# Output projection of a gated attention and feed-forward kernel: fp32r products with TensorE transposes, against scaled fp16 products with transposing DMAs

## The chip, the cores and the metric

The kernel runs on one core of one Trainium2 chip. The metric is device time in microseconds, the median of several runs. Besides the runs there is one profiled execution with a trace of every instruction and DMA packet; its own time is given below. TensorE multiplies matrices, VectorE, ScalarE and GpSimd work elementwise, and SyncE's queue issues nearly all DMAs. Profiles name them PE (PEld for its weight loads), DVE, ACT, POOL and SP. A matmul reads its operands from SBUF and accumulates in one of eight PSUM banks.

## The reference

With S = 2048 tokens, D = 576 channels, 32 heads of 18 channels, four segments of 512 tokens and F = 4608 hidden channels:

```python
g = sigmoid((x * gate_w).sum(-1, keepdims=True))
# attention branch: per segment, causal softmax attention inside the segment and a running
# memory (M, z) of the segments before; sb = sigmoid(beta), one per head
o = sb * (phi(q) @ M) / (phi(q) @ z + 1e-6) + (1 - sb) * softmax(q k^T * scale + mask) @ v
a = o @ wo
b = (silu(x @ w_gate) * (x @ w_up)) @ w_down      # feed-forward branch
out = g * a + (1 - g) * b
```

Everything is fp32 in the reference. The kernel keeps near that precision by splitting each operand into a high and a low part in a short format and adding three products (high x high, high x low, low x high).

## The kernel before, in words

**Stages.** First come the projections q, k, v and the memory branch, segment by segment; the memory branch's rows (already weighted by sigmoid(beta)) go to a DRAM array `med`, one row of 576 per token. Then the feed-forward branch runs for the two halves of the tokens (`half` 0 and 1), each over 36 tiles of hidden channels (`f`), so 72 *positions*; the attention of 64 units of two heads is woven into it and writes its rows to the DRAM array `atd`. Last comes the output stage: for 16 tiles of 128 tokens, in the order segments 2, 3, 0, 1, it forms o = `atd` + `med` (segment 0 has no `med`), multiplies by `wo`, and merges with the feed-forward rows.

**A position of the feed-forward loop.** Seven groups of seven matmuls (`seven`, lines 1388 and 1391) with steps of ScalarE and VectorE between them. L1471 copies the first group's PSUM bank for further accumulation, L1494 is a SiLU, L1500 and L1501 multiply gate and up parts, L1260 and L1263 split the result in `hh` and `hl` for the down projection. After each group, and one extra time, stands a `tick`, eight a position, numbered 0 to 7. A tick issues DMAs of its own (`dw`, line 1149), then one *beat*: it runs whatever was deferred to this beat, then some down-projection groups (9 matmuls each, line 1160, accumulated on VectorE at L1169), then a step of the attention. `defer(k, fn)` puts a function into the k-th beat from now. Down groups come in sixteens after every third f, so positions come in threes: one long, with the groups, and two short. The sixteen groups of the last three f are left over for the output stage. Weights for the next position (line 864, `wo__` tiles of a pool, not the matrix wo) and their remainder (line 355) are fetched through SyncE's queue one position ahead.

**Queues.** The order on every engine and queue is the program's order, written out by hand; no scheduler moves it. An instruction whose inputs are not ready holds what is behind it on its engine. This holds for SyncE's queue too: a DMA that waits for its source or for a free buffer holds the DMAs behind it. In the second half the attention turns part of its units with transposing DMAs (`turn`, line 950), of 128 x 1024 fp16, in that same queue.

**Opening the output stage.** When the attention is through, in beat 6 of the third position from the end, `c_open` closes its pools and opens the pool `cp`. It spreads six loads of parts of `wo` (line 1204, into the four staging buffers of `raw_tile`) over the next nine beats; five beats after each load ScalarE copies the high part (L1207), seven beats after, VectorE takes the low part (L1208), which frees the staging buffer. `c_load` (lines 1213, 1217) fetches `atd` and `med` rows of tile 0 in beat 2 and of tile 1 in beat 6.

**The output stage.** Seventeen rounds (line 1538). Round n loads tile n+2 and its feed-forward rows (`f_load`, for tiles 0 to 7; the others are still in SBUF), prepares tile n (`c_tr`), runs two left-over down groups (four in round 0), and multiplies tile n-1: for each half of 288 output channels `products` runs 14 matmuls (line 223), one down group follows if there is one, and VectorE scales the feed-forward rows (L1554) and adds the product times the gate (L1555). The finished rows are stored one round later (line 1558), the last tile's by halves (line 1560).

`c_tr` adds the two rows on GpSimd (L1229), copies the last 64 channels once more beside them (L1230), turns the row tile on TensorE with five transposes (L1233, L1235) into PSUM, and splits that in fp32r with ScalarE (L132, L252) and VectorE (L133, L253):

```python
nc.tensor.transpose(ta[:, k], o[:, P * k:P * k + P], idt)   # k = 0..3
nc.tensor.transpose(tb, o[:, 512:640], idt)
split(oh, ol, ta)
xs_split(os_, tb)
```

The last 64 channels need only two products: their high part fills one half of the partitions, their low part the other.

## Time and profile before

| what | value |
|---|---|
| median of 3 runs | 1737.57 us (1737.48 to 1737.6) |
| profiled execution, its own time | 1739.27 us |
| its span, first to last instruction | 1737.6 us |
| TensorE busy | 1687.6 us |
| VectorE, ScalarE, GpSimd busy | 1354.4, 1067.6, 880.1 us |
| mean granted TensorE clock | 0.996 |
| bytes moved by DMA | 311.30 MB |

How to read the lines below: a group line names source line, engine, operation, output and inputs, count, busy time, mean length of one in ns and the engine's idle time before it with what ended it. A timeline line gives start, length, engine, line, and in brackets the idle time before. In the chain of waits each piece has start, length and what held the end of the program at that time. A line on a stretch of time gives the busy time of each engine in it, the granted clock, the share of the 16 DMA engines' time and GB/s. A busy TensorE is not a TensorE at its peak, because matmuls overlap; the distance from start to start tells the pace.

### The profile page before, as it was taken

To read this page: it belongs to the slowest core of one execution; us is meant where nothing else is said; L and a number is where in the kernel's file an instruction comes from. 1 tells how busy PE (TensorE), PEld (TensorE's weight loads), DVE (VectorE), ACT (ScalarE), POOL (GpSimd) and SP (SyncE) were. 2 spreads that over 40 slices of the span, in tenths; PEclk is the share of its full clock that TensorE was granted. 3 is DMA by queue.
4 is the path that set the end of the run, shared out by engine and by line. 5 is a ranking of instruction groups with operands and counts; after the bars stand their busy time and mean duration, and the time that the engine had idled before them with its cause. 6 is when DMAs were issued, how large, how long until landed. Compare 5 with 4: busy or idle time off the path is not lost.

```text
span 1737.6 us, 35226 instructions
## 1 busy us (share of the span) xinstructions
PE 1687.6 (97%) x12267; PEld 1094.3 (63%) x12267; DVE 1354.4 (78%) x3299; ACT 1067.6 (61%) x1906; POOL 880.1 (51%) x1187
## 2 busy tenths in 40 slices
PE   9999989999999999999999999999999999999999
PEld 7888865556555655555555556556656656665599
DVE  7677666789888988888885888788878788875565
ACT  7656568677777777667764665664655466565411
POOL 3326552256567655664552665465546565553121
PEclk9999999999999999999999999999999999999999
DMA  8666676665776675536534476775676578654544
GB/s 286 219 219 216 213 243 212 201 203 169 236 223 197 180 238 188 156 114 193 170 100 158 136 169 139 182 193 138 144 200 169 130 176 189 158 124 133 169 146 137
DMA packets 341670, 311.30 MB, mean 179 GB/s; under 512 B 193396, under 2 KB 258676, under 8 KB 341492
## 3 DMA queue, kind: packets, MB, share of 16 engines
q1 hardware_dynamic: 341492, 309.05, 61.5%
q8 instruction: 96, 1.57, 0.4%
q14 instruction: 82, 0.67, 0.1%
HBM read 183.20 MB, written 99.55 MB: 163 GB/s over the span
## 4 chain that ended last, share of the span: by engine, by line
PE 63%; DVE 12%; ACT 11%; POOL 5%; issue 4%; DMA 4%; SPq 1%; DVEq 0%; ACTq 0%; POOLq 0%
PE bank L1388 24%; PE bank L1160 18%; PE bank L223 7%; PE bank L1391 4%; PE bank L889 3%; PE bank L1000 2%; POOL ws L369 2%; PE bank L1028 1%; ACT L1492 1%; ACT row L1492 1%; DVE ya L1169 1%; DVE junk L907 1%; ACT row L1494 1%; ACT L1381 1%; ACT dw L1137 1%
## 5 line engine op out<-in xcount | busy, mean ns | idle before, releaser
L1160 PE MATMUL bank<-dw,hh 128*128 128x320 f16 (+1 forms) x2304 | 438.1, 286 | 17.3 <-DVE ya L1169 13.3
L1160 PE MATMUL bank<-dw,hl 128*128 128x320 f16 (+1 forms) x1152 | 330.1, 287 | 2.8 <-DVE hl L1263 2.2
L1104 POOL TENSOR_TENSOR p<-pe,p 128x512 f16<-128x512 f32 x220 | 271.3, 1233 | 75.9 <-DVE p L1100 46.0
L1160 PEld LDWEIGHTS <-hh 128*128 128x128 f16 x2304 | 224.8, 98 | 105.6 <-issue 22.6
L1004 ACT ACTIVATE pe<-bank 128x512 f32<-128x512 f32 x220 | 130.1, 592 | 187.9 <-PE bank L1000 174.7
L1169 DVE SCALAR_TENSOR_TENSOR ya<-bank,sc,ya 128x320 f32<-128x320 f32 x352 | 176.2, 511 | 54.1 <-PE bank L1160 52.0
L1391 PE MATMUL bank<-xr,rh 128*128 128x512 f16 x504 | 191.3, 379 | 3.2 <-DMA rh<-rc 3.2
L907 DVE CUSTOM_DVE_ANT_0 junk<-bank,cm 128x128 bf16<-128x128 f32 (+2 forms) x352 | 169.4, 481 | 14.0 <-PE bank L889 9.2
L1263 DVE SCALAR_TENSOR_TENSOR hl<-hh,row 128x512 f16<-128x512 f16 x144 | 128.9, 896 | 49.3 <-ACT hh L1260 48.2
L1012 POOL TENSOR_SCALAR_AFFINE_SELECT pe<-pe 128x256 f32<-128x256 f32 (+1 forms) x220 | 90.3, 411 | 151.5 <-ACT pe L1004 146.7
L1160 PEld LDWEIGHTS <-hl 128*128 128x128 f16 x1152 | 112.6, 98 | 35.4 <-DVE hl L1263 5.2
L889 PE MATMUL bank<-kst,qst 108*128 108x512 bf16 (+3 forms) x512 | 124.5, 299 | 6.5 <-ACT pe L1004 4.9
L1000 PE MATMUL bank<-qst,kst 111*128 111x512 bf16 (+3 forms) x352 | 103.2, 300 | 0.7 <-DVE acc L973 0.7
L369 POOL TENSOR_TENSOR ws<-raw 128x256 f32<-128x256 f32 x72 | 66.1, 919 | 72.7 <-DMA raw<-in_wf_dram 30.1
L1100 DVE CAST p<-pe 128x512 f16<-128x512 f32 x203 | 102.4, 505 | 0.0
L1490 DVE TENSOR_TENSOR row<-bank,row 128x512 f32<-128x512 f32 x72 | 49.7, 690 | 61.0 <-ACT bank L1489 60.7
L223 PE MATMUL bank<-xo,qhi 128*128 128x512 f32 x288 | 93.7, 406 | 0.1
L466 POOL TENSOR_TENSOR q<-qr,q 128x512 bf16<-128x512 f32 x36 | 47.9, 1331 | 87.8 <-ACT q L465 81.0
L1260 ACT ACTIVATE hh<-row 128x512 f16<-128x512 f32 x144 | 89.1, 619 | 4.0 <-DVE row L1500 3.1
L1485 ACT ACTIVATE row<-bank 128x512 f32<-128x512 f32 x72 | 43.0, 597 | 76.8 <-PE bank L1391 76.4
L1391 PEld LDWEIGHTS <-rh 128*128 128x128 f16 x504 | 49.4, 98 | 63.3 <-issue 4.2
L1471 ACT ACTIVATE bank<-bank 128x512 f32<-128x512 f32 x72 | 41.9, 582 | 73.6 <-PE bank L1391 60.8
(1090 smaller groups left out, 4233.4 us busy)
## 6 DMA issues: line engine op xcount, KB each, us to landing
xo<-in_wf_dram SPq DMA_DIRECT2D x65, 320.0 KB
raw<-in_wf_dram SPq DMA_DIRECT2D x72, 256.0 KB
dc<-dw SPq DMA_DIRECT2D x36, 432.0 KB
dw<-dc SPq DMA_DIRECT2D x36, 432.0 KB
rh<-rc SPq DMA_DIRECT2D x72, 168.0 KB
draw<-in_wd_dram SPq DMA_DIRECT2D x36, 288.0 KB
xo<-in_xT_dram SPq DMA_DIRECT2D x33, 256.0 KB
vd<-vps SPq DMA_DIRECT2D x8, 912.0 KB
```

Source lines behind the costliest of these rows:

```text
L223: nc.tensor.matmul(t, st[n], mv[n], start=(n == 0), stop=(n == 13))
L889: nc.tensor.matmul(t[:, c:c + w], qs[:KR, pr, P * i:P * i + P], ks[:KR, pr, 0:w], start=True, stop=True)
L907: nc.vector.tensor_tensor_reduce(junk.bitcast(BF)[:, :w], t[:, c:c + w], cm[:, L - w:L], 1.0, -3.0e38, OP.add, OP.max, m[:, k:k + 1])
L1000: nc.tensor.matmul(t[:, c:c + w], ks[:KR + 3, pr, P * j:P * j + P], qs[:KR + 3, pr, P * j:L], start=True, stop=True)
L1004: nc.scalar.activation(pe, t, AF.Exp, scale=SCALE)
L1100: nc.vector.tensor_copy(p1, pe)
L1104: nc.gpsimd.tensor_sub(p2, pe, p1)
L1160: nc.tensor.matmul(t, p, d[:, q, cs], start=(f == CH * c and n == 0), stop=(f == CH * c + CH - 1 and n == 2))
L1169: nc.vector.scalar_tensor_tensor(ya[:, i, cs], t, inv[c], ya[:, i, cs], op0=OP.mult, op1=OP.add)
L1263: nc.vector.scalar_tensor_tensor(lo, hi, -STEP, src, op0=OP.mult, op1=OP.add)
L1388: nc.tensor.matmul(t, w[:, p, z], x[z][:, q], start=first and n == 0, stop=False, skip_group_check=True)
L1391: nc.tensor.matmul(t, rem[:, RPOS[j]], XR[j], start=False, stop=True, skip_group_check=True)
```

## The change

The output projection is computed from fp16 terms, and its rows are split before they are turned.

- **Scale.** fp16 has a narrow range, so both operands are brought to a scale. In half 1, positions f = 8 to 13, `o_scan` loads `wo` and `wv` in twelve parts through SyncE into the `raw` staging buffers and ScalarE squares and sums each, four beats after its load. At f = 16 `o_scale` adds the sums (VectorE), spreads them over partitions with one small matmul, and forms powers of two: column 12 scales `wo`, column 13, together with the largest norm of x (column 126, written by `reach`), scales the rows; their product's reciprocal goes into the gate `gg`.
- **Weights.** `wo` is split in fp16 with that scale; VectorE's step is a scalar_tensor_tensor instead of a subtraction.
- **Rows.** `c_sum` (GpSimd adds `med`), `c_high` (ScalarE, 576 columns to fp16), `c_low` (VectorE, two pieces) work on the row tile in token order, and `c_turn` turns the 128 x 1152 fp16 result with one transposing DMA in SyncE's queue. TensorE's transposes and the GpSimd copy are gone.
- **Order.** `c_open` now puts loads of tiles 0 to 3 in beats 2, 6, 10, 14 and sum, high part, low part and turn of tiles 0 to 2 in the four beats from 6, 10 and 14. The output stage has sixteen rounds; round n turns tile n+2, loads tile n+4, sums and splits tile n+3, and multiplies tile n.

```diff
     def reach(t):
...
-        nc.vector.tensor_reduce(xq, sc[:, 0:4], axis=AX.X, op=OP.max)
-        nc.vector.tensor_scalar(xq, xq, sx, sx, op0=OP.mult, op1=OP.mult)
+        nc.vector.tensor_reduce(column(126), sc[:, 0:4], axis=AX.X, op=OP.max)
+        nc.vector.tensor_scalar(xq, column(126), sx, sx, op0=OP.mult, op1=OP.mult)
...
-                wos.append(cps[0].tile([P, 2, NT, 288], F32R, name=f"wo{hf}", bufs=1))
+                wos.append(cps[0].tile([P, 2, NT, 288], F16, name=f"wo{hf}", bufs=1))
...
-            defer(2, lambda: tiles.update({0: c_load(0)}))
-            defer(6, lambda: tiles.update({1: c_load(1)}))
+            for n in range(4):
+                defer(2 + 4 * n, lambda n=n: c_load(n))
+                if n < 3:
+                    for k, fn in enumerate((c_sum, c_high, c_low, c_turn)):
+                        defer(6 + 4 * n + k, lambda fn=fn, n=n: fn(n))
...
-            defer(n + 5, lambda: nc.scalar.activation(wos[hf][:, 0, :, c], box[0], AF.Copy))
-            defer(n + 7, lambda: nc.vector.tensor_sub(wos[hf][:, 1, :, c], box[0], f32(wos[hf][:, 0, :, c])))
+            k = column(12)
+            defer(n + 5, lambda: nc.scalar.activation(wos[hf][:, 0, :, c], box[0], AF.Copy, scale=k))
+            defer(n + 7, lambda: nc.vector.scalar_tensor_tensor(wos[hf][:, 1, :, c], box[0], k, wos[hf][:, 0, :, c],
+                                                                op0=OP.mult, op1=OP.subtract))
+
+        def o_scan(k):
+            w, c = divmod(k, 6)
+            src, c, box = (wo, wv)[w], slice(96 * c, 96 * c + 96), []
+
+            def load():
+                box.append(raw_tile()[:, :96 * NT])
+                nc.sync.dma_start(box[0].rearrange("p (k n) -> p k n", n=96), src[:, :, c])
+
+            return [(0, load), (4, lambda: square(box[0], k, junk[:, :96 * NT]))]
+
+        def o_scale(k):
+            z = sc[:, 12:14]
+            if k == 0:
+                total(column(12), 0, 6)
+                total(column(13), 6, 12)
+                t = ts_tile([P, 2])
+                across(t, z)
+                nc.vector.tensor_scalar_max(z, t, FLOOR)
+                nc.gpsimd.tensor_scalar_mul(column(13), column(13), column(126))
+            elif k == 1:
+                grade(z, z)
+                nc.vector.tensor_scalar_mul(z, z, TOP)
+                nc.gpsimd.tensor_mul(column(14), column(12), column(13))
+            else:
+                nc.vector.reciprocal(column(14), column(14))
+                nc.gpsimd.tensor_scalar_mul(gg, gg, column(14))
...
+        def c_sum(n):
+            o, me = tiles[n][:2]
+            if me is not None:
+                nc.gpsimd.tensor_add(o, o, me)
+
+        def c_high(n):
+            t = tiles[n][2] = cps[0].tile([P, 9 * P], F16, name="oq")
+            nc.scalar.activation(t[:, 0:D], tiles[n][0], AF.Copy, scale=column(13))
+
+        def c_low(n):
+            o, t = tiles[n][0], tiles[n][2]
+            for c, a, b in ((D, 512, D), (640, 0, 512)):
+                nc.vector.scalar_tensor_tensor(t[:, c:c + b - a], o[:, a:b], column(13), t[:, a:b],
+                                               op0=OP.mult, op1=OP.subtract)
+
+        def c_turn(n):
+            t = tiles[n][3] = cps[0].tile([P, 9, P], F16, name="ok", bufs=4)
+            nc.sync.dma_start_transpose(t, tiles[n][2])
...
+            if FT + 8 <= pos < FT + 14:
+                for k in range(2):
+                    plan += [(4 * k + o, fn) for o, fn in o_scan(2 * (pos - FT - 8) + k)]
+            if pos == FT + 16:
+                plan += [(2 * k, lambda k=k: o_scale(k)) for k in range(3)]
...
+        for n in range(16):
+            if n and n + 2 < 16:
+                c_turn(n + 2)
+            if n + 4 < 16:
+                c_load(n + 4)
+            if n + 2 < 16:
+                ffs[n + 2] = f_load(n + 2)
+            if n + 3 < 16:
+                for fn in (c_sum, c_high, c_low):
+                    fn(n + 3)
+            downs(2 if n else 4)
+            ops = c_side(n)
```

`c_side` hands out the nine turned blocks: four high, one of both parts of the last 64 channels, four low.

More of the change, by code (lines that the diff above doesn't have):

```diff
@@ L1217, in c_load @@
                 nc.sync.dma_start(me, med[tt])
-            return o, me
+            tiles[n] = [o, me, None, None]
+        def c_sum(n):
[13 more added lines that the diff above has]
+            nc.sync.dma_start_transpose(t, tiles[n][2])
         def f_load(n):
@@ L1225, in f_load, with c_side @@
             return ff
[L1227 to L1240 removed]
+        def c_side(n):
+            t = tiles.pop(n)[3]
             r = []
             for k in range(4):
[L1243 to L1244 removed]
+                r += [t[:, k], t[:, 5 + k], t[:, k]]
+            return r + [t[:, 4], t[:, 4]]
         stores = []
@@ L1525, in gated_mix @@
         sent = []
-        ops = None
         def downs(k):
```

63 lines of the change are left out of this document (19 added, 44 removed).

## The prediction

> **What bounds the kernel now.** I read the page's busy row first, then the busy time by stretch, then the chain of waits.
>
> ```profile
> PE 1687.6 (97%) x12267; PEld 1094.3 (63%) x12267; DVE 1354.4 (78%) x3299; ACT 1067.6 (61%) x1906; POOL 880.1 (51%) x1187
> ```
>
> ```profile
> core 0: us, PE busy (x) PEld busy (x) DVE busy (x) ACT busy (x) POOL busy (x), PEclk, DMA share, GB/s
> ...
> 1564.00:1566.00 2.00, 2.00 (x19) 1.65 (x18) 1.63 (x9) 0.60 (x1) 0.97 (x3) 1.00 1.15 257
> 1647.80:1734.20 86.40, 85.93 (x670) 81.63 (x668) 51.86 (x100) 13.40 (x34) 18.53 (x24) 1.00 0.44 146
> ...
> 1630.00:1640.00 10.00, 9.63 (x45) 4.05 (x43) 5.30 (x8) 6.84 (x12) 2.02 (x3) 1.00 1.05 314
> ...
> 1091.80:1230.00 138.20, 137.37 (x1086) 81.56 (x1084) 113.02 (x313) 84.96 (x143) 78.92 (x106) 1.00 0.72 175
> ```
>
> TensorE sets the time at the full granted clock: it is busy in 137.37 of 138.20 us where the scans will stand, and in 85.93 of 86.40 us of the output stage, where VectorE (51.86) and the DMA engines (0.44) have room. Only around 1630 are the DMA engines full (1.05). The chain gives TensorE's pace (start, length, what):
>
> ```profile
> 1560.38 2.21 PE bank L1160 x18
> ...
> 1722.42 3.72 PE bank L223 x28
> 1726.14 0.44 PE bank L1233 x4
> 1726.58 0.11 PE bank L1235
> 1726.69 7.46 PE bank L223 x56
> 1734.17 0.52 DVE ya L1555
> ```
>
> One token tile of the projection is 28 matmuls in 3.72 us, its five transposes stand before it in the same row of work for 0.44 + 0.11 = 0.55 us, and nothing lies between. The stage adds up: 16 tiles x 3.72 = 59.5, 15 sets of transposes x 0.55 = 8.3, 16 left-over down groups at 2.21 / 2 = 1.1 are 17.7; together 85.5 of 86.4.
>
> **The change part by part.**
>
> *Transposes off TensorE.* 15 x 0.55 = 8.3 us leave the path. The sixteenth set (the first) ran at 1647.4, where TensorE next waits for `hl` anyway (row at 1650.20 below), so it gives nothing. Each transpose is 272 ns long by its own row, but five take 0.55:
>
> ```profile
> L133 DVE TENSOR_TENSOR ol<-bank,oh 128x512 fp32r<-128x512 f32 x16 | 11.1, 691 | 7.0 <-ACT oh L132 7.0
> ...
> L1233 PE MATMUL bank<-idt,o 128*128 128x128 f32 x64 | 9.6, 272 | 0.0
> ...
> L132 ACT ACTIVATE oh<-bank 128x512 fp32r<-128x512 f32 x16 | 9.6, 599 | 65.1 <-PE bank L1233 65.1
> ...
> L253 DVE TENSOR_TENSOR os<-bank,os 64x128 fp32r<-64x128 f32 x16 | 4.7, 295 | 0.5
> ```
>
> The Trainium skill, "TensorE: Matmul & The Clock Gate", Part 4 (PE-mode transpose), prices one at about 275 ns in a kernel's context; the trace agrees on the length (272) but not on what it occupies. By that price the 75 transposes of the 15 sets would give 75 x 0.275 = 20.6 us instead of 8.3, and the time would be some 12 us lower than my sum. That case gets no chance: the chain's rows count from start to start.
>
> *Products in fp16.* The x18 row is fp16 matmuls of 320 and 256 columns in equal parts, 288 on average, each with its own weights: 2.21 / 18 x 28 = 3.44 us a tile against 3.72, so 16 x 0.28 = 4.5 us. Bounds: nothing, if fp16 at 288 columns kept the old pace; 4.5 if the row carries over, which I take, since mean width and weight loads are the same.
>
> *The tile's split.*
>
> ```profile
> L1260 ACT ACTIVATE hh<-row 128x512 f16<-128x512 f32 x144 | 89.1, 619 | 4.0 <-DVE row L1500 3.1
> ```
>
> By this row and the ones above, ScalarE gives up 0.60 and a smaller copy and gets one copy of 576 columns (0.62 x 576 / 512 = 0.7); VectorE gives up 0.69 and 0.29 and gets a pair of like size (about 0.98); GpSimd loses a small copy. Beside 86 us of TensorE all of it is covered by VectorE's free 34 us. It costs something only through order, which is the next two points.
>
> *The last two positions and the start of the stage.* `c_open` now puts the split of tiles 0 to 2 and their transposing DMAs into the last two positions of the feed-forward loop. What stands there now:
>
> ```profile
> 1636.42 0.67 ACT L1494 ACTIVATE row<-bank,sc 128x512 f32<-128x512 f32 x1
> 1636.99 1.08 ACT L1207 ACTIVATE wo<-raw 128x480 fp32r<-128x480 f32 x2
> 1638.40 0.58 ACT L1471 ACTIVATE bank<-bank 128x512 f32<-128x512 f32 x1 [0.33 <-PE bank L1391]
> ```
>
> ```profile
> 1636.55 0.75 DVE L1500 SCALAR_TENSOR_TENSOR row<-bank,sc,row 128x512 f32<-128x512 f32 x1 [1.08 <-ACT row L1492]
> ...
> 1647.63 0.75 DVE L1500 SCALAR_TENSOR_TENSOR row<-bank,sc,row 128x512 f32<-128x512 f32 x1 [0.60 <-PE bank L1391]
> ```
>
> ```profile
> 1638.56 0.55 SPq L1204 DMA_DIRECT2D raw<-in_wo_dram  x1
> 1639.15 0.63 SPq L864 DMA_DIRECT2D wo__22174<-wc  x1
> ...
> 1641.72 0.61 SPq L1217 DMA_DIRECT2D me<-med  x1
> ...
> 1714.79 0.45 SPq L1217 DMA_DIRECT2D me<-med  x1
> ```
>
> ```profile
> 1645.84 1.46 PE L1388 MATMUL bank<-xo,wo__22174 128*128 128x512 f16 x6
> ...
> 1650.20 0.31 PE L1160 MATMUL bank<-dw,hl 128*128 128x320 f16 x1 [0.40 <-DVE hl L1263]
> ```
>
> ```profile
> 1647.55 1.41 POOL L1229 TENSOR_TENSOR o<-o,me 128x576 f32<-128x576 f32 x1 [5.56 <-DMA me<-med]
> ...
> 1718.46 1.43 POOL L1229 TENSOR_TENSOR o<-o,me 128x576 f32<-128x576 f32 x1 [2.35 <-DMA me<-med]
> ```
>
> `c_high(0)` comes behind the weight copy that starts at 1636.99, so it ends near 1638.2. `c_low(0)` stands on VectorE ahead of the gating step L1500, which moves from 1636.55 to about 1639.2. L1500 reads the bank that L1471 of the last position writes, so L1471 goes from 1638.40 to 1640, and TensorE, which accumulates on what L1471 read, stands about 0.8. The last weight load waits for a staging buffer that VectorE frees behind L1500, so SyncE gets to it at about 1641 instead of 1638.56. Behind it now stand `c_turn(0)` and both loads of tile 2, ahead of the weights wo__22174, which go out near 1644.7 instead of 1639.15 and are wanted at 1646.6: another 0.4 or so. A `me` load lands and wakes GpSimd 3.2 us after its issue ends in the half-empty stage (1715.24 to 1718.46), 5.2 in the full one (1642.33 to 1647.55). With the shorter, tile 2 is summed by 1648.7, copied by 1649.4, and its `c_low(2)` ends at 1650.4, ahead of the last L1500, which ran at 1647.63. So `hl`, for which TensorE waits at 1650.20, comes 2.7 us later, and the earlier stands lie inside that. I take 2.7; low end 0.5 (only the transposes that filled the wait are missed), high end 5 (the longer landing).
>
> *The loop through SyncE's queue in the stage.* Order there: `c_turn(n+2)`, the loads of tile n+4, then the store of n-1. A transposing DMA holds the queue far longer than a plain one:
>
> ```profile
> L950 SPq DMA_TRANSPOSE xo<-xo x100: 1231/1262/3862, 990.7 to 1567.2; - x100
> L1213 SPq DMA_DIRECT2D o<-atd x16: 319/378/587, 1627.8 to 1714.4; - x16
> ```
>
> Nine blocks instead of eight: 1.26 x 9 / 8 = 1.42 us. From one turn to the turn two tiles later: 1.42 + 0.44 + 0.45 for the loads, 3.2 landing, 1.43 sum, 0.7 copy, 0.98 low part, 0.3 of hand-overs: 8.9 us, against two steps of 3.44 = 6.9. Without a `me` (tiles 8 to 11) it is 8.9 - 0.45 - 1.43 - 0.5 = 6.5, which fits. Tiles 4 to 7 are prepared in steps that left-over groups stretch to 5.6 and more. So only tiles 12 to 15 lag, 2 us each round, two interleaved rounds. A lagging `c_low` holds the accumulation of the tile three before it and so a PSUM bank; that hand-over has some 0.2 us left after the first round, and the second round's 2 us go onto the path. I take 2.0; low end 0, high end 8 (landing 5.2: rounds 2 x 4 and 2 x 1.6 too long, less some 3 of lead). In DMA time a turn is dear too:
>
> ```profile
> 1561.13 3.20 SPq L950 DMA_TRANSPOSE xo<-xo  x2
> ```
>
> In the stretch after these two, 1564 to 1566, the DMA engines moved 257 GB/s at a share of 1.15, against 314 at 1.05 around 1630 to 1640, where transfers are plain: a third more time per byte; nine blocks are about 1.3 us in a step of 3.44 in which two loads and a store take about 1 us each by the 314. Hidden, just.
>
> *Scans in the main loop.* Twelve loads of 240 KB on SyncE and twelve squares on ScalarE in six positions near 1100 to 1215. A square costs 616 + 186 ns at 512 columns, so 0.77 at 480, 9.2 us in all, in a stretch where ScalarE is busy 84.96 of 138.20.
>
> ```profile
> L140 ACT ACTIVATE xr<-xr x6: 612/616/617, 64.5 to 117.0; 128x512 f32<-128x512 f32 x6
> L140 ACT ACTIVATION_READ_ACCUMULATOR xr<-xr x6: 184/186/187, 65.0 to 117.5; 128x1 f32 x6
> ```
>
> ```profile
> 1208.87 5.21 SPq L950 DMA_TRANSPOSE xo<-xo  x2
> 1214.13 0.57 SPq L864 DMA_DIRECT2D wo__16205<-wc  x1
> ```
>
> The danger is a square that waits for its load and holds ScalarE's evacuations. It stands four beats behind the load.
>
> ```profile
> 1209.56 1.46 PE L1388 MATMUL bank<-xo,wo__15860 128*128 128x512 f16 x6
> ...
> 1214.99 1.46 PE L1388 MATMUL bank<-xo,wo__16134 128*128 128x512 f16 x6
> ```
>
> In the last of these positions the second load would go out after the group at 1209.56 and its square come after the one at 1214.99, so at 1216.5, 5.4 us on. SyncE is held by two transposes until 1214.1; a load behind them lands near 1217.4 (0.5 issue, the shorter landing of 3.2 less a little), about 1 us late. I take 1.5 for the stage; bounds 0 and 12 x 1.3 = 16. The scale itself (one small matmul, eight small steps, three on GpSimd) is some 0.2 us each beside TensorE; if TensorE had to wait for one, under 1. The stores' order and the last two stores do not move: after TensorE's end the same accumulation and store follow.
>
> Sum: 8.3 + 4.5 - 2.7 - 2.0 - 1.5 = 6.6 us. The profiled execution took 1739.27 (span 1737.6 and 1.67 around it): 1732.7. The median of the runs, 1737.57, lies 1.7 below it, so I predict 1731.0.
>
> **The rivals.**
>
> *All hidden.* The start loses 0.5, nothing else: 12.3 gained, 1725.3. For it: room on VectorE and the DMA engines. Against it: queue orders above.
>
> *The queue's loop sets the stage's step.* Landing at 5.2 throughout: start 5, loop 8, scans 1.5: 14.5 lost for 12.8, so 1739, no change. For it: the full DMA engines at 1630 to 1640. Against it: a share of 0.44 in the stage. The Trainium skill, "VectorE: DVE Perf Modes", Rules for kernel authors, says to transpose 128 x 128 on TensorE if PSUM will do and to use the DMA only otherwise, which is what this change reverses. By the same page's 1309 ns for one block (The three transpose paths) nine would take 11.8 us a tile and the stage would be over 100 us longer; the eight-block issue of 1.26 us here is against that figure.
>
> *Scans hold ScalarE: slower.* If every square came 1.3 us late, as I reckon for one, 16 us go instead of 1.5: 1745.5. It decides from 12 x 0.7 us on. Against it is all that TensorE waits for from 1091.8 to 1230, 0.8 us, none of it for a DMA, though SyncE issues weights in the same positions:
>
> ```profile
> PE bank L1160 <- DVE ya L1169: 0.8, 2, 0.6
> ```
>
>
> *No faster products.* fp16 at the old pace: 4.5 less, 1735.5.
>
> **How the numbers follow.** Under 0.2% (3.5 us) a run of this kernel can't be told from no change. My sum with 4 to 10 us gained: 0.45; all hidden 0.2; the queue's loop 0.15; scans 0.12; no faster products 0.08. Faster by over 0.2%: 0.42 + 0.2 + 0.05 + 0.02 + 0.01 = 0.7; within: 0.03 + 0.08 + 0.07 = 0.18; slower: 0.02 + 0.10 = 0.12. The range runs from all hidden less a little, 1724.5, to the queue's loop, 1739, and leaves out most of the scans' case. My sum's own range is 1727 to 1734.
>
> **What would show it.** In the profile after: L223's 28 matmuls in 3.44 us without L1233 between; `hl`'s wait at the stage's start grown from 0.4 to about 3; a few waits of L223 on VectorE's accumulation in the last five tiles; ScalarE waiting for `raw` from the scan loads, rarely over 1 us. Waits of L223 on `ok` would say that the turns land late; gaps of L1388 behind ScalarE around 1100 to 1215 would make me wrong on the slow side.

## The result, and the profile after

| | before | after |
|---|---|---|
| median | 1737.67 us (20 runs) | 1740.76 us (20 runs, 1737.66 to 1744.65) |
| profiled execution: span | 1737.6 us | 1741.0 us |
| mean granted TensorE clock | 0.996 | 0.996 |

The ratio is 1.0015, with a 95% interval of 1.0008 to 1.0021: the changed kernel is slower by 0.15%. The forecast was 1731.0 and faster. The time is outside the range of 1724.5 to 1739.0.

In the new source the lines of the feed-forward loop lie 36 to 44 lower: the groups of seven stand on L1427 and L1430 (1388 and 1391 before), the copy of the bank on L1515 (1471), the gate products on L1544 and L1545 (1500, 1501), `hh` and `hl` on L1299 and L1302 (1260, 1263). L1169 is the down projection's accumulation as before. New are the row steps: `c_sum` L1255, `c_high` L1259, `c_low` L1264, `c_turn` L1269, the loads L1245 (`o`) and L1249 (`me`), and the merge of the output L1601 and L1602.

The page's busy row first, then the busy time by stretch (columns as before: stretch, length, busy time of each engine with its instructions, granted clock, DMA share, GB/s):

```profile
PE 1676.7 (96%) x12189; PEld 1069.8 (61%) x12189; DVE 1352.3 (78%) x3307; ACT 1074.4 (62%) x1914; POOL 875.6 (50%) x1174
```

```profile
core 0: us, PE busy (x) PEld busy (x) DVE busy (x) ACT busy (x) POOL busy (x), PEclk, DMA share, GB/s
1091.80:1230.00 138.20, 133.91 (x1062) 79.50 (x1061) 108.70 (x305) 87.30 (x161) 75.88 (x103) 1.00 0.79 188
1648.00:1738.00 90.00, 79.86 (x620) 60.19 (x618) 52.27 (x105) 16.70 (x24) 14.02 (x10) 1.00 0.83 218
1650.00:1660.00 10.00, 7.16 (x42) 3.68 (x41) 6.84 (x12) 5.11 (x9) 1.99 (x2) 1.00 1.11 266
1670.00:1690.00 20.00, 20.00 (x166) 16.01 (x164) 13.44 (x26) 2.33 (x3) 4.21 (x3) 1.00 0.60 174
1700.00:1710.00 10.00, 10.00 (x84) 8.00 (x82) 6.21 (x13) 1.55 (x2) 0.00 (x0) 1.00 1.02 260
```

TensorE lost 10.9 us of work (1687.6 to 1676.7), and yet the span grew by 3.4. So idle time grew by some 14 us. Two stretches hold it. Where the scans stand, TensorE was busy for 137.37 of 138.20 us before and is for 133.91 now. In 90 us of the output stage it is idle for 10.1. The list of what TensorE waited for from 1600 to the end (total us, times, longest) names the second part:

```profile
PE bank L223 <- DVE ya L1602: 4.9, 4, 1.5
PE bank L223 <- DVE ya L1169: 2.2, 1, 2.2
PE bank L1427 <- ACT bank L1515: 1.5, 1, 1.5
PE bank L1427 <- DMA wo__22235<-wc: 1.4, 1, 1.4
PE bank L1160 <- ACT hh L1299: 1.2, 1, 1.2
PE bank L1160 <- DVE hl L1302: 0.3, 1, 0.3
```

Before, two waits of 0.4 us were all from 1590 on. To compare the stretches of different kernels I take the starts of single matmuls from each trace. *Loop* is from the first matmul of position 44 (f = 8 of the second half, the first with a scan) to that of position 70, the last but one; *opening* is from the first matmul of position 71 to that of the last group of seven; *stage* is from the first matmul of position 71 to the last one of the projection.

| kernel | loop | opening | stage |
|---|---|---|---|
| before | 533.78 | 9.14 | 97.15 |
| after | 538.67 | 12.23 | 95.86 |

The loop lost 4.9 us. The stage, in which 12.8 us less of TensorE work stands by the prediction, gained 1.3. Position 70 itself takes 10.58 instead of 11.12, position 44 starts 0.6 later, and the end after the last product is some 0.2 shorter; together, before rounding, that is the growth of the span.

**The opening.** The timeline of the kernel after, all engines, cut to the steps that hold the next one:

```profile
1643.97 0.95 DVE L1264 SCALAR_TENSOR_TENSOR oq<-o,sc,oq 128x64 f16<-128x64 f32 x2 [3.14 <-ACT oq L1259]
...
1644.84 0.74 DVE L1544 SCALAR_TENSOR_TENSOR row<-bank,sc,row 128x512 f32<-128x512 f32 x1
...
1645.67 0.58 ACT L1515 ACTIVATE bank<-bank 128x512 f32<-128x512 f32 x1 [1.15 <-DVE row L1544]
...
1648.07 1.38 SPq L1269 DMA_TRANSPOSE ok<-oq  x1
...
1650.64 0.43 SPq L864 DMA_DIRECT2D wo__22235<-wc  x1
...
1654.20 0.45 SPq L1249 DMA_DIRECT2D me<-med  x1
...
1655.89 0.95 DVE L1264 SCALAR_TENSOR_TENSOR oq<-o,sc,oq 128x64 f16<-128x64 f32 x2 [2.24 <-ACT oq L1259]
...
1656.76 0.74 DVE L1544 SCALAR_TENSOR_TENSOR row<-bank,sc,row 128x512 f32<-128x512 f32 x1
...
1657.54 1.29 ACT L1299 ACTIVATE hh<-row 128x512 f16<-128x512 f32 x2 [1.68 <-DVE row L1544]
...
1658.95 0.31 PE L1160 MATMUL bank<-dw,hl 128*128 128x320 f16 x1 [0.28 <-DVE hl L1302]
...
1659.41 1.40 POOL L1255 TENSOR_TENSOR o<-o,me 128x576 f32<-128x576 f32 x1 [4.36 <-DMA me<-med]
...
1660.85 0.78 ACT L1259 ACTIVATE oq<-o,sc 128x576 f16<-128x576 f32 x1 [2.02 <-POOL o L1255]
...
1661.65 0.95 DVE L1264 SCALAR_TENSOR_TENSOR oq<-o,sc,oq 128x64 f16<-128x64 f32 x2 [2.11 <-ACT oq L1259]
...
1662.52 1.79 DVE L1169 SCALAR_TENSOR_TENSOR ya<-bank,sc,ya 128x320 f32<-128x320 f32 x4
...
1663.97 0.41 PE L223 MATMUL bank<-wo,ok 128*128 128x288 f16 x2 [2.18 <-DVE ya L1169]
```

`c_low(0)` holds VectorE until 1644.84, so L1544 is late, ScalarE's copy L1515 waits 1.15 us for it, and TensorE stands 1.46. The first turn and the loads of tile 2 stand in SyncE's queue before the weights `wo__22235`, which go out at 1650.64, and TensorE stands 1.37. `c_low(2)` (1655.89) waits 2.24 us for the rows of tile 2, the last L1544 stands behind it, and `hh` waits 1.68 us for that. `hl` is there 27.86 us after the start of position 70 (1631.09), where it was 24.63 before (1625.57 to 1650.20): 3.2 us. Then comes what the sum did not have: `c_sum(3)` waits on GpSimd for a `me` that was issued at 1654.20 and lets GpSimd go only at 1659.41, so `c_high(3)` and `c_low(3)` end only at 1662.6. The accumulations of the first left-over down groups (L1169) stand behind `c_low(3)` on VectorE, so no bank is free, and the first product of the stage waits 2.18 us.

**The late rounds.** TensorE's own timeline there, and the steps before one of its waits:

```profile
1714.92 3.59 PE L223 MATMUL bank<-wo,ok 128*128 128x288 f16 x28 [1.54 <-DVE ya L1602]
1719.95 3.59 PE L223 MATMUL bank<-wo,ok 128*128 128x288 f16 x28 [1.45 <-DVE ya L1602]
1724.23 3.59 PE L223 MATMUL bank<-wo,ok 128*128 128x288 f16 x28 [0.68 <-DVE ya L1602]
1729.07 6.16 PE L223 MATMUL bank<-wo,ok 128*128 128x288 f16 x49 [1.26 <-DVE ya L1602]
```

```profile
1709.72 1.12 SPq L1245 DMA_DIRECT2D o<-atd  x1
...
1710.89 0.43 SPq L1249 DMA_DIRECT2D me<-med  x1
...
1712.86 0.95 DVE L1264 SCALAR_TENSOR_TENSOR oq<-o,sc,oq 128x64 f16<-128x64 f32 x2 [4.08 <-ACT oq L1259]
...
1714.35 0.94 DVE L1602 SCALAR_TENSOR_TENSOR ya<-bank,gg,ya 128x288 f32<-128x288 f32 x2
...
1715.66 1.40 POOL L1255 TENSOR_TENSOR o<-o,me 128x576 f32<-128x576 f32 x1 [3.64 <-DMA me<-med]
```

The chain of waits (start, length, what), whose long pieces from 1650 on were all TensorE's in the kernel before, now runs over landings of 2.8 to 4.6 us:

```profile
1689.18 2.79 DMA o<-atd
...
1710.89 4.61 DMA me<-med
```

The 28 matmuls of a tile take 3.59 us with the pipeline's end, and before each of four of the last tiles stands a wait of 0.68 to 1.54 us for L1602, the merge of an earlier tile. L1602 runs late since it stands behind a `c_low` on VectorE, which waits for a sum, which waits for loads that stand in the queue behind a turn. The `me` issued at 1710.89 let GpSimd start at 1715.66, 4.3 us after its issue ended.

### The profile page after: what moved, and what is told of

It is laid out like the page before. It is cut to its first block, busy times and chain, and to the rows that moved or that the text cites. A ratio compares the mean times of both kernels' runs of the same rounds, so it can differ in the third digit from the quotient of the medians.

```text
span 1741.0 us, 35135 instructions
## 1 busy us (share of the span) xinstructions
PE 1676.7 (96%) x12189; PEld 1069.8 (61%) x12189; DVE 1352.3 (78%) x3307; ACT 1074.4 (62%) x1914; POOL 875.6 (50%) x1174
## 4 chain that ended last, share of the span: by engine, by line
PE 59%; DVE 13%; ACT 13%; issue 5%; POOL 4%; DMA 4%; SPq 2%; POOLq 0%; DVEq 0%; ACTq 0%
PE bank L1427 23%; PE bank L1160 18%; PE bank L223 5%; PE bank L1430 4%; PE bank L889 3%; PE bank L1000 2%; ACT L1536 1%; PE bank L1028 1%; ACT row L1536 1%; DVE ya L1169 1%; POOL ws L369 1%; ACT row L1538 1%; DVE junk L907 1%; ACT L1420 1%; ACT dw L1137 1%
## 5 line engine op out<-in xcount | busy, mean ns | idle before, releaser
L1004 ACT ACTIVATE pe<-bank 128x512 f32<-128x512 f32 x220 | 130.1, 592 | 188.8 <-PE bank L1000 174.8
L1169 DVE SCALAR_TENSOR_TENSOR ya<-bank,sc,ya 128x320 f32<-128x320 f32 x352 | 176.1, 511 | 52.7 <-PE bank L1160 50.8
L1430 PE MATMUL bank<-xr,rh 128*128 128x512 f16 x504 | 191.3, 380 | 2.3 <-DMA rh<-rc 2.3
L1302 DVE SCALAR_TENSOR_TENSOR hl<-hh,row 128x512 f16<-128x512 f16 x144 | 127.6, 887 | 49.4 <-ACT hh L1299 48.3
L223 PE MATMUL bank<-xo,qhi 128*128 128x512 f32 x288 | 93.7, 406 | 0.1
L1299 ACT ACTIVATE hh<-row 128x512 f16<-128x512 f32 x144 | 89.1, 619 | 3.6 <-DVE row L1544 3.2
L1430 PEld LDWEIGHTS <-rh 128*128 128x128 f16 x504 | 49.4, 98 | 62.5 <-issue 3.3
L1515 ACT ACTIVATE bank<-bank 128x512 f32<-128x512 f32 x72 | 41.9, 581 | 74.0 <-PE bank L1430 54.8
```

The lines of the kernel that those rows point to most:

```text
L223: nc.tensor.matmul(t, st[n], mv[n], start=(n == 0), stop=(n == 13))
L1004: nc.scalar.activation(pe, t, AF.Exp, scale=SCALE)
L1169: nc.vector.scalar_tensor_tensor(ya[:, i, cs], t, inv[c], ya[:, i, cs], op0=OP.mult, op1=OP.add)
L1302: nc.vector.scalar_tensor_tensor(lo, hi, -STEP, src, op0=OP.mult, op1=OP.add)
L1430: nc.tensor.matmul(t, rem[:, RPOS[j]], XR[j], start=False, stop=True, skip_group_check=True)
```

## The experiments

All times are medians in us; the ratio is to runs of the kernel before that were taken beside them, whose medians lay between 1737.03 and 1737.77.

| kernel | median | ratio, 95% interval | loop | opening | stage |
|---|---|---|---|---|---|
| e1_noscan | 1737.02 | 1.0003 [0.9994, 1.0013] | 533.76 | 13.04 | 97.05 |
| e2_inplace | 1739.6 | 1.0012 [1.0003, 1.0021] | 537.94 | 12.62 | 95.84 |
| e3_loads_first | 1735.43 | 0.9991 [0.9981, 1.0001] | 538.57 | 13.67 | 95.30 |
| e4_pe_transposes | 1737.04 | 0.9998 [0.9989, 1.0008] | 538.58 | 9.15 | 93.07 |
| e5_scan_loads_only | 1736.16 | 0.9989 [0.9979, 0.9999] | 534.06 | 12.32 | 97.19 |
| e6_scan_middle | 1742.22 | 1.0028 [1.0018, 1.0038] | 538.88 | 12.68 | 95.21 |
| e7_split_after | 1744.55 | 1.0031 [1.0019, 1.0042] | 538.62 | 9.16 | 98.69 |
| e8_deep_loads | 1734.93 | 0.9983 [0.9974, 0.9992] | 538.66 | 13.51 | 91.15 |
| e9_hybrid | 1731.71 | 0.9961 [0.9947, 0.9975] | 538.57 | 9.16 | 85.44 |
| e10_scan_vector | 1740.1 | 1.0016 [1.0007, 1.0025] | 536.70 | 12.45 | 97.78 |
| e11_hybrid_vector | 1729.3 | 0.9956 [0.9942, 0.997] | 537.66 | 9.07 | 85.35 |
| e12_hybrid_noscan | 1725.8 | 0.9929 [0.9915, 0.9943] | 533.78 | 9.13 | 86.03 |

The first 1090 us are the same code in all of them but do not take the same time in each profiled execution: position 44 starts at 1091.79 before, 1092.41 after, and between 1085.31 and 1090.73 in those of the twelve others. Single runs of one kernel spread over some 4 to 9 us. That is why the stretches carry the argument, and the medians only confirm it; the loop without squares came out at 533.76 to 534.06 four times.

**Half clock behind waits.** TensorE's granted clock is 1.00 nearly everywhere in these traces, but 0.50 in single stretches of 3.4 us. Before position 44 there are four of them in the kernels before and after and none in e11, which gets there 6.5 us earlier than the kernel before. No loop has one. From position 70 to the last product there is one in e1, e8 and e10, there are two in e3, one of 6.8 us stands in e7, and the others have none. Each begins inside a wait of TensorE of 2.0 to 6.6 us or at most 1.1 us behind it. Here is the second one of e3, then that of e8:

```profile
1719.00:1722.40 3.40, 3.40 (x17) 2.10 (x15) 3.30 (x6) 0.78 (x1) 1.42 (x1) 0.50 0.82 198
1653.80:1657.20 3.40, 3.40 (x14) 1.90 (x13) 2.92 (x6) 1.26 (x2) 0.14 (x1) 0.50 1.15 279
```

In e3's stretch 17 matmuls ran, where 28 fit at the full granted clock (3.43 us, worked out below), so such a stretch costs up to 1.7 us besides the wait, an estimate from half the clock. It is in the stage column: without it the stage would be about 95.4 in e1, 91.9 in e3, 89.4 in e8, 96.1 in e10, and, since matmuls ran in 3.94 us of its 6.8, 96.7 in e7. A wait of 2.6 us in e5 has no such stretch behind it, so the length of the wait alone does not decide; what does was not tested.

**How much one execution can say of the stage.** The kernel after, e1, e2, e5, e6 and e10 have the same output stage. It took 95.21 to 97.78 us in them, and the waits for L1602 were 4.3 to 5.6 us. Smaller differences of a stage say nothing.

### What in the scans costs: e1, e2, e5

e1 leaves out the scans:

```diff
-            if FT + 8 <= pos < FT + 14:
-                for k in range(2):
-                    plan += [(4 * k + o, fn) for o, fn in o_scan(2 * (pos - FT - 8) + k)]
...
+                nc.gpsimd.memset(column(12), 2.0 ** 10)
+                nc.gpsimd.memset(column(13), 2.0 ** 7)
```

> The twelve scan loads and squares are left out; fixed powers of two stand in for the scales (2^10 for the weights, 2^7 for the rows). Theory (the scans hold the feed-forward loop back): the second-last position starts near 1625.6 as before the change, not 1631.1, and the time is 5 us under the changed kernel's, near 1735.5. Rival (the 5.5 us come from elsewhere, the scans cost what was taken for them): 1.5 us under, near 1739.3.

e2 keeps them but squares in place:

```diff
-            return [(0, load), (4, lambda: square(box[0], k, junk[:, :96 * NT]))]
+            return [(0, load), (4, lambda: square(box[0], k))]
```

> The squares write back into their staging buffer instead of the shared tile junk, into which VectorE's row maxima (L907) write too. Theory (VectorE waits for ScalarE over junk): L907's waits for L140 go, 3 to 4 us less than the changed kernel, near 1737. Rival (ScalarE's time or SyncE's queue is what the scans cost): under 1 us less, near 1740.5.

e5 keeps the loads and leaves out squares and sums:

```diff
-            return [(0, load), (4, lambda: square(box[0], k, junk[:, :96 * NT]))]
+            return [(0, load)]
```

> The scan loads stay, the squares and the sums are left out; fixed powers of two stand in for the scales. Measured from the start of the position with f = 8 to that of the second-last one, 533.8 us before, 538.7 in the changed kernel, 533.8 without scans. Theory (the squares' time on ScalarE is what costs): 534. Rival (SyncE's queue and the DMA engines carry the cost): 538.

e1's time of 1737.02 lies between the theory's 1735.5 and the rival's 1739.3, e2's 1739.6 nearer to its rival. The loop is back at 533.76 without the scans and at 534.06 with their loads alone; in place it is 537.94. So of the 4.9 us the loads cost 0.3 and the shared scratch tile 0.7. The rest, some 4, is that of the squares and of the scale, which e5 leaves out as well; the scale's position (52) alone lost 0.5. The stretch of the scans in e5 shows TensorE as busy as before, though the loads are there (DMA share 0.82, 196 GB/s):

```profile
1091.80:1230.00 138.20, 137.38 (x1118) 82.16 (x1117) 112.39 (x313) 84.93 (x144) 79.61 (x106) 1.00 0.82 196
```

None of the squares waited for its load: in the profile of the kernel after ScalarE has no wait for `raw` there. What they cost is their own time on ScalarE, by the rows of their line (shortest, median and longest of the twelve, ns):

```profile
L140 ACT ACTIVATE junk<-raw x12: 580/594/597, 1102.1 to 1222.9; 128x480 f16<-128x480 f32 x12
L140 ACT ACTIVATION_READ_ACCUMULATOR junk<-raw x12: 185/192/194, 1102.6 to 1223.4; 128x1 f32 x12
```

That is 0.78 us each, 9.4 in all, of which 4.9 / 12 = 0.4 us each reach TensorE, with the loads and the scale counted in.

### Whether the place matters, or the engine: e6, e10

e6 spreads the same scans over one position of each three (f = 7, 10, 13, 16, 19, 22):

```diff
-            if FT + 8 <= pos < FT + 14:
-                for k in range(2):
-                    plan += [(4 * k + o, fn) for o, fn in o_scan(2 * (pos - FT - 8) + k)]
-            if pos == FT + 16:
+            if FT + 7 <= pos < FT + 25 and pos % 3 == 1:
+                for k in range(2):
+                    plan += [(4 * k + o, fn) for o, fn in o_scan(2 * ((pos - FT - 7) // 3) + k)]
+            if pos == FT + 25:
```

> The same scans, two a position, but only in the middle one of each three positions (f = 7, 10, 13, 16, 19, 22; the scale at f = 25). Theory (a square costs only where down groups and their accumulation follow; the middle positions lost nothing in the changed kernel): the loop loses under 1 us, the second-last position starts 4 to 5 us earlier against the start of f = 7, the time is near 1736.5. Rival (every square costs its 0.4 us wherever it stands): no gain, near 1740.5.

My theory fell. By single positions of the kernel after, only some had lost time (1.2 to 1.6 us in the positions 45, 47 and 48, 0.5 at the scale in 52, nothing in 46 and 49), and I had read that as a matter of place. Since e6 starts one position earlier it is compared from position 42 to 70: 587.97 us, against 582.87 before and 587.77 after. The loss is the same elsewhere: 5.1 us here and 4.9 there.

e10 leaves the scans where they were and makes the sums of squares on VectorE:

```diff
-            return [(0, load), (4, lambda: square(box[0], k, junk[:, :96 * NT]))]
+            return [(0, load), (4, lambda: nc.vector.tensor_tensor_reduce(
+                junk[:, :96 * NT], box[0], box[0], 1.0, 0.0, OP.mult, OP.add, sc[:, k:k + 1]))]
```

> The kernel after with one edit: the twelve sums of squares are made on VectorE in one multiply-and-add pass each instead of on ScalarE. Theory (it is ScalarE's order that counts: its copies of the banks stand in the loop's path, about 0.4 us of each 0.77 us square reaches TensorE; VectorE's steps come later in the row of work and have slack): start of position 44 to start of position 70 533.8 to 535.5 us, time 1736.5 to 1738. Rival (any engine in this loop passes such an insert on, and VectorE is the busier one, 113.02 of 138.20 us): 538 us or more, time 1740 to 1742.

The loop took 536.70, between the two theories: 2.9 us lost where ScalarE lost 4.9. The time, 1740.1, lies in the rival's range, but the stage of this execution holds a stretch at half clock. Here are VectorE's two rows for the scans (instructions, busy us, mean ns), then the stretch:

```profile
L1223 DVE CUSTOM_DVE_ANT_0 junk<-raw 128x480 f16<-128x480 f32 x12 | 9.1, 760 | 0.0
...
L1223 DVE DVE_READ_ACCUMULATOR2_ANT sc<- 128x1 f32 x12 | 0.9, 78 | 0.0
```

```profile
1091.80:1230.00 138.20, 136.09 (x1074) 80.51 (x1073) 120.78 (x336) 82.72 (x140) 80.04 (x104) 1.00 0.78 191
```

VectorE gets 10.0 us of work in the stretch where it was the busier engine already, and passes on 0.24 us of each 0.83. The same edit in e11 lost 3.9, so the gain over ScalarE is one to two us and not well settled. From 1091 to 1300, TensorE waits for ScalarE's copies in the kernel after (L1515 1.1 us, L1004 1.0), which it does not in the kernel before, and 2.9 us instead of 1.6 for the accumulations on L1169; with the sums on VectorE only the latter remain (2.6). These waits are a part of the loss. Where the rest arises, and why one place passes on more than another, is open.

### The products alone: e4

e4 has the fp16 products and the scans, but the five transposes stay on TensorE, and the fp16 parts are split out of PSUM:

```diff
+        def c_tr(n):
...
+            for k in range(4):
+                nc.tensor.transpose(ta[:, k], o[:, P * k:P * k + P], idt)
...
+            split_16(oh, ol, ta, column(13))
...
-                if n < 3:
-                    for k, fn in enumerate((c_sum, c_high, c_low, c_turn)):
-                        defer(6 + 4 * n + k, lambda fn=fn, n=n: fn(n))
```

> fp16 products with scans and scale, but the rows are turned by TensorE as before and split out of PSUM; no transposing DMAs, no early split. Theory: 28 products take 3.44 us, 4.5 us gained over 16 tiles, the scans' 5.5 lost, nothing else moves: near 1738.5. Rival (fp16 at 288 columns keeps the old pace): near 1743.

The opening is that of before (9.15), the stage is 4.1 us shorter, and the loop is 4.8 longer; the time is that of before, 1.5 us under the theory's 1738.5. TensorE is busy in all of its stage but 1.1 us:

```profile
1640.00:1730.00 90.00, 88.90 (x706) 69.98 (x705) 59.86 (x107) 21.90 (x44) 20.96 (x26) 1.00 0.51 168
```

### The order in SyncE's queue: e3, e8

e3 puts the loads of a round ahead of its turn:

```diff
-            if n and n + 2 < 16:
-                c_turn(n + 2)
             if n + 4 < 16:
                 c_load(n + 4)
             if n + 2 < 16:
                 ffs[n + 2] = f_load(n + 2)
+            if n and n + 2 < 16:
+                c_turn(n + 2)
```

> In each round of the output stage the loads go into SyncE's queue ahead of the transposing DMA. Theory (loads stand behind the turn, a loop of about 8.9 us over two rounds): the products' waits for VectorE's accumulation in the last five tiles fall from 4.9 to under 1 us, near 1736.5. Rival (the DMA engines are full, share 0.96 to 1.02 from 1690 to 1710, and loads land late in any order): these waits stay over 3 us, near 1740.

e8 keeps that order and also loads up to six tiles ahead (the edit against e3):

```diff
-            if n + 4 < 16:
-                c_load(n + 4)
+            for z in {0: (4,), 1: (5, 6), 2: (7, 8)}.get(n, (n + 6,)):
+                if z < 16:
+                    c_load(z)
...
-            o = cps[0].tile([P, D], F32, name="o", bufs=3)
+            o = cps[0].tile([P, D], F32, name="o", bufs=6)
...
-                me = cps[0].tile([P, D], F32, name="me", bufs=3)
+                me = cps[0].tile([P, D], F32, name="me", bufs=6)
...
-            t = tiles[n][2] = cps[0].tile([P, 9 * P], F16, name="oq")
+            t = tiles[n][2] = cps[0].tile([P, 9 * P], F16, name="oq", bufs=3)
```

> Loads ahead of the turn and up to two rounds further ahead (six row buffers), three buffers for the split rows. Theory (the late rounds want more DMA time than they last, share 1.0 to 1.17 from 1690 to 1720, while the rounds with left-over groups leave a third free): the products' wait for VectorE's accumulation, 4.9 us in the changed kernel and 2.7 with loads first, falls under 0.5 and the time is near 1734. Rival (the order behind the turn is all): no better than loads first, near 1735.5.

What TensorE waited for from 1590 on, in e3 and then in e8:

```profile
PE bank L1427 <- DMA wo__22235<-wc: 2.8, 1, 2.8
PE bank L223 <- DVE ya L1602: 2.7, 1, 2.7
```

```profile
PE bank L1427 <- DMA wo__22235<-wc: 2.7, 1, 2.7
PE bank L223 <- DVE ya L1169: 1.6, 1, 1.6
```

The order alone takes the waits of the late rounds from 4.9 to 2.7, between theory and rival, and with the loads earlier they are gone; from the first product to the last it is 73.56 us after, 72.58 in e3 and 68.23 in e8. e3's 72.58 holds a stretch at half clock; its profiled execution, 1740.21, was the slowest of eleven. So what the late rounds lacked was the loads' lead. The DMA engines have time for the stage as a whole: the early rounds of the kernel after left them at a share of 0.60 (1670 to 1690 above). And in e8 they are no emptier from 1690 to 1720 (shares of 1.06 to 1.11) than in the kernel after (0.96 to 1.02), yet no product waits there for a merge. e8 also has a third buffer for the split rows, whose part was not tested alone. The opening keeps its waits in both, with a longer one for the weights (2.8 and 2.7). That is not the edits' order, since `wo__22235` goes out 8.97 to 8.98 us into position 71 in all three, behind the same DMAs; why it landed later is open.

### The opening: e7, e9

e7 moves the sum, split and turn of tiles 0 to 2 behind the loop:

```diff
-                if n < 3:
-                    for k, fn in enumerate((c_sum, c_high, c_low, c_turn)):
-                        defer(6 + 4 * n + k, lambda fn=fn, n=n: fn(n))
...
         sent = []
+        for n in range(3):
+            for fn in (c_sum, c_high, c_low, c_turn):
+                fn(n)
```

> Sum, high and low part and turn of tiles 0 to 2 stand behind the feed-forward loop instead of in its last two positions; four row buffers instead of three, no other change. Theory (the early low parts hold VectorE's gating step and the early turns hold SyncE's fetch of the last weights): the waits of the last position (1.5 for ScalarE, 1.4 for the weights, 1.5 for hh and hl) go; the first product comes later against the last weights, but 3 us earlier than in the changed kernel against the second-last position: near 1737.5. Rival (the rows' own chain of sum, split and turn is what is late, wherever it stands): no gain, 1740.5 or more.

```profile
PE bank L223 <- DVE ya L1169: 6.6, 1, 6.6
PE bank L223 <- DVE ya L1602: 4.4, 4, 1.3
```

The opening is 9.16, as before the change, but the rows are now so late that the first product waits 6.6 us for an accumulation that stands behind their splits on VectorE. The stage is 2.8 us longer than with the split in the last two positions, some 2.0 of it by the half clock at the end of the wait (the estimate above). Moving the work did not help, as the rival had it; in both places tried, the rows' chain of load, sum, split and turn was too long for the first tiles.

e9 therefore turns the first four tiles on TensorE, as e4 does, and only tiles 4 to 15 by DMA, with loads ahead of the turns and up to five tiles early:

```diff
+        K = 4
+        c_load(2)
+        nxt = c_tr(0)
+        downs(4)
         for n in range(16):
...
+            for z in {0: (3, 4), 1: (5,), 2: (6, 7)}.get(n, (n + 5,)):
+                if z < 16:
+                    c_load(z)
...
+            if K <= n + 2 < 16:
+                c_turn(n + 2)
...
+            ops = nxt if n < K else c_side(n)
+            if n + 1 < K:
+                nxt = c_tr(n + 1)
```

> Both halves of the two ways: the first four tiles are turned on TensorE as before (fp16 parts out of PSUM, no early split in the last positions), tiles 4 to 15 by the transposing DMAs, with loads ahead of the turn in SyncE's queue and five buffers. Theory (the gain of the change is whole, and what takes it back is three separate things: squares, the early split in the last positions, and loads queued late behind the turns): start of position 71 to the last group of seven as before, 9.1 to 9.3 us; the stage from position 71 to the last product 87 to 89 us against 97.15 before, less than in any kernel so far; the loop still 4.9 longer; time some 4 to 5 us below before, 1732 to 1734. Rival (the early split is not the cause, the opening only moves its waits: SyncE's queue must still issue the same DMAs and tiles 4 to 6 lack their lead): the waits of L223 for VectorE come back at tiles 4 to 6, 3 us or more, stage 91 or more, time 1736 to 1738.

The stage in e9, as a whole and then in three pieces:

```profile
1634.00:1724.00 90.00, 89.85 (x681) 66.43 (x679) 59.61 (x113) 25.36 (x41) 18.65 (x16) 1.00 0.81 232
1684.00:1694.00 10.00, 10.00 (x84) 7.98 (x82) 6.68 (x16) 1.80 (x3) 0.00 (x0) 1.00 1.14 285
1694.00:1704.00 10.00, 10.00 (x84) 7.98 (x83) 7.66 (x16) 2.07 (x3) 2.81 (x2) 1.00 1.22 297
```

TensorE is idle for 0.15 us in 90, and no wait of its is left in the stage. The whole stage takes 85.44 us, 11.7 less than before and better than the 87 to 89 expected. The terms of the prediction give 12 x 0.55 + 4.5 = 11.1 for it, since four sets of transposes stay, of which the first had cost nothing. With the squares still in the loop the kernel takes 0.9961 of the time before.

### Both together, and without the scans: e11, e12

e11 is e9 with e10's edit, e12 is e9 with e1's.

> The two edits together: the first four tiles turned on TensorE and the rest by DMAs with early loads, and the sums of squares on VectorE. Theory (the two gains lie in different stretches and add): start of position 44 to position 70 536.7 us, position 71 to the last product 85.4; the profiled stretches give 1.9 us less than with the squares on ScalarE, time 1729 to 1731. Rival (VectorE's insert shows only by the chance of one execution): 538.5 us again, time 1731 to 1733.

> The hybrid without the scans (loads and squares left out, fixed powers of two as scales, so nothing fits itself to the inputs' size). Theory (what is left then is the output stage alone): position 44 to 70 533.8, position 71 to the last product 85 to 86 against 97.15 before, together some 11.5 us under before, time 1726 to 1728, that is all that the prediction summed as gain without its costs. Rival (without the squares TensorE runs ahead and meets late weights or landings instead, as the opening did when the scans were left out of the kernel after): the stage 88 or more, time 1729 to 1731.

e12 has the loop of before (533.78) and a stage of 86.03: 11.1 us less, and 11.2 in the median. That is what the change can give where nothing takes it back, but its scales are fixed numbers. e11 computes everything, with scales from the norms, and has the lowest ratio of the kernels that do, 0.9956; e9's 0.9961 lies within its interval. Its loop, 537.66, is again between theory and rival.

## Why the prediction was wrong

**Transposes off TensorE, products in fp16: right.** The pace of 3.44 us for 28 matmuls came out: the 49 of the last row of TensorE's timeline take 6.16, and 28 take 3.59, so 21 more take 2.57, 0.1224 each, and 28 x 0.1224 = 3.43. And e4, which has only this gain, has a stage shorter by 4.1 where 4.5 was said. The sum of both terms stands in e9 and e12 as worked out above. The rival without faster products is out.

The Trainium skill, "VectorE: DVE Perf Modes", Rules for kernel authors, says to transpose on TensorE if PSUM will do. As the change was built the rule held: e4's stage of 93.07 us, with transposes on TensorE, beats the 95.86 of the kernel after. With loads in time the measurement speaks against it, since twelve tiles by DMA and four on TensorE take 85.44.

**Scans in the main loop: the step that failed most, 1.5 predicted, 4.9 measured.** I looked for a square that waits for a late load, and took it that squares in time are covered, because ScalarE was busy for only 84.96 of 138.20 us. No square waited for its load, and without squares and scale (e5) the loss is gone. A square delays what stands behind it on ScalarE by 0.78 us whether or not ScalarE is idle at another time, and TensorE, at 137.37 of 138.20, has almost no slack that could take it up. About half of the squares' time came through. The waits for L1515 and L1004 agree with this way; only a part of the loss was followed to single waits. The rival in which the scans hold ScalarE had the right engine and a price of 16 us, by the wrong mechanism.

**The last two positions and the start of the stage: 2.7 predicted, 5.4 measured.** The queue order was right, to the place: L1544 behind `c_low(0)` and again behind `c_low(2)`, L1515 behind the first, `wo__22235` behind the turn and the loads of tile 2, `hl` late by 3.2 where 2.7 was said. What failed is the end of that step: I followed tile 2 to its `c_low(2)` and stopped. Tile 3's is not part of `c_open` but of round 0, where it stands ahead of the accumulations that free the banks, and its load was in the full DMA engines (266 GB/s at 1.11 between 1650 and 1660). With it the first product waits for 2.2 more.

**The loop through SyncE's queue: mechanism and place right, size off.** The waits of L223 behind L1602 stand at the last tiles, four of them, as said. I took 2.0, by landings of 3.2 us, as in the stage before, whose DMA share was 0.44. The share after is 0.83, and the late `me` landed in 3.4 to 4.3 us. Turns between 1696 and 1708 took 2.0 to 2.1 us where I had 1.42, and a load of `o` behind one 1.12 where I had 0.44. The 4.9 lies about midway between the value taken and the range's end of 8, with landings of 5.2. One sum of mine contradicts its own conclusion: a turn of 1.3 us of DMA time and three plain transfers of about 1 us are 4.3 in a step of 3.44, which is not "hidden, just". By it, loads issued in a late round had to land late. That the loads' place is the cause is shown by e3, where the order alone takes away 2.2 of the 4.9, and by e8, where the rest goes with their lead.

The sum as it was: 12.8 gained, less 5.4, 4.9 and 4.9, is 2.4 lost. From position 44 on the two profiles differ by 2.9, so some 0.5 is not assigned. Each of the three costs was two to over three times what I took, all to the same side. Two of them I had priced by an average share, ScalarE's in the loop and the DMA engines' in the old stage, and the third by following the chain one tile too short.

## What to carry to other kernels

Where one engine is busy for 99% of a stretch, an instruction put on another engine is not free merely because that engine idles 40% of the time: what counts is what stands behind it in its own order, and here 30 to 50% of such an insert came through. When transposes move from the matrix engine to DMAs, give the loads that feed them a lead of several tiles and put them ahead of the turn in the queue, and keep the first tiles, which can have no lead, on the old path. Follow a moved chain past the last item that the edit names, to the first one that the next loop takes over. And count a wait of TensorE at more than its length where a stretch at half clock can follow it, 1.7 us here.

## What the runs showed of the hardware

The transposing DMAs are slow to issue (shortest, median, longest, in the kernel after and then in e9):

```profile
L1269 SPq DMA_TRANSPOSE ok<-oq x16: 1249/1408/2100, 1648.1 to 1728.1; - x16
```

```profile
L1288 SPq DMA_TRANSPOSE ok<-oq x12: 1252/1543/2287, 1666.3 to 1711.8; - x12
```

A plain load of `o` took 0.38 us in the kernel before (median); behind a turn in the late rounds shown above one took 1.12. I had reckoned with 1.42 for a turn; the median after is 1.41, but single ones took up to 2.29. In the kernel after the turns issued at a DMA share of up to 0.56 took 1.25 to 1.38 us, those at 0.84 to 1.13, 1.43 to 2.10; in e9 the link is looser (1.43 at 1.24). The Trainium skill, "Advanced Engine Details and Errata", X-Bar Transpose (TRN2), says that transposing DMAs are as fast as regular ones. That isn't borne out by these traces: by time on the engines, 10 us of the kernel after with turns, loads and stores moved 260 GB/s at a share of 1.02 (1700 to 1710), where plain transfers moved 314 at 1.05 in the kernel before. By packets of these 10 us, the turns' 256 bytes took 25 ns on average, 0.10 ns a byte, and the rows' 2304 bytes 118 ns, 0.05 a byte. Plain packets of 384 bytes took 24 ns around 1630 before, so how much is the turning and how much the small packet stays open.

A DMA share above 1 was no bound by itself. In e9 the DMA engines stood at 1.14 and 1.22 for 20 us, with a turn of 2.22 us among them, and TensorE lost nothing; the loads had been issued up to five tiles before.
